# Finer loads of one weight group, one exp moved behind a copy, eight small loads moved one slab on: three edits to a fused attention and feed-forward kernel

## The chip, the cores and the metric

The kernel runs on one core of one Trainium2 chip. The metric is the device time of one execution in microseconds (us). Times are medians of several runs, and ratios carry a 95% interval. The profile comes from one execution, and its times count from the start of that execution's span.

## The reference, cut to what matters

```
q_s = softmax(q, over the head dimension);  k_s = softmax(k, over the sequence)
kv  = einsum('bhsd,bhse->bhde', k_s, v)            # 64 x 64 per head
x   = einsum('bhsd,bhde->bhse', q_s, kv)           # 8 batches x 576 tokens x 512
h   = x @ w_in                                     # 512 -> 2048
out = (h * sigmoid(beta * h)) @ w_out              # 2048 -> 512
```

The shapes are 8 batches, 8 heads, 576 tokens, 64 per head, all float32. The kernel computes in bf16 with float32 sums. It works in nine slabs of 512 tokens: the first 512 tokens of each batch, then the eight remainders of 64 together.

## The kernel before

PE is the matmul engine, ACT does exp and some copies, DVE and POOL do casts, sums and scaling, and SP issues nearly all loads in one queue. A helper turns recorded operations into five instruction streams and puts in the semaphore waits; each stream runs in the order in which the program adds to it. Names in the profile lines: QF, KF and VF are queries, keys and values as loaded, EQ and EK their exps, VB the cast values, QT the transposed queries, KVC the key-value products; XT is the attention output, the input of the first layer; O2S and WST are staging buffers, WIN and WOUT the weights in bf16, GT the hidden layer, PS the banks that take PE's sums, and QRF and EQR belong to the remainder queries.

The weights of the first layer come in four column groups `c` of four row blocks `m`. They land in float32 staging buffers and are cast to bf16:

```
for c in range(4):
    for m in range(0, NM, 1 if c < 2 else 2):
        load_win(c, m, 1 if c < 2 else 2)          # groups 0, 1: 256 KB; groups 2, 3: 512 KB
...
def cast_win(c, m, eng):
    add(eng, lambda e: e.tensor_copy(WIN[:, m, 512 * c:512 * c + 512], STAGE[c][:, m, :]),
        r=[SKEY[c][m]], w=[("win", c, m)])
```

While slab 0 is in its second layer, batch 1 is prepared for slab 1. A list of pieces of work is put between the matmuls, each at a given slot:

```
todo = [(107, lambda: go(t_steps(1, (0, 1), (1,), ACTE))),            # transposes of queries
        (107.1, lambda: cast_v(1, 0, ACTE)),
        (111.1, lambda: scale_wout(14, 2)), (119.1, lambda: (exp_kc(1, 2), exp_kc(1, 3))),
        (118, lambda: kv_half(1, (7, 0), 0)),
        (124, lambda: out_half(1, (1, 2), 0)), (124.5, evacs)]         # copies to XT 0 and 1
... # then slab 1 begins:
at(0, 0, 3)               # three matmuls with XT block 0
kv_half(1, (7, 0), 2)     # 36 small key-value products of the last two head pairs
at(1, 0, 3)
at(0, 3, 5)
out_half(1, (7, 7, 7, 0), 2)
```

`exp_kc(1, 3)` is the exp of batch 1's last keys. `out_half` ends with the two copies XT<-PS, block 0 on DVE and block 1 on ACT. The remainder queries of two batches come in eight loads of 32 KB (`load_qrem`). Two such sets are issued in slab 1, ahead of the store of slab 1 and the loads of batch 4:

```
for hp in range(2, 4):
    norm_main(2, hp, 1, POOL if hp == 2 else DVE)
t_dma(2, 2, 2)
load_qrem(2)
load_qrem(0)
```

The softmax here doesn't subtract the row's maximum and nothing guards it: scores larger than these inputs give would overflow.

## Time and profile before

| | before |
|---|---|
| time, median of the first 3 runs | 280.04 us (279.76 to 280.06) |
| span of the profiled execution | 278.2 us |
| PE busy | 273.0 us (98%) |
| first weight matmul of slab 0 | 13.62 us |
| matmul after the 36 products | 45.48 us |

The matmul lengths are modelled, so a busy PE has to be read from starts: in an unbroken stretch, 512-column matmuls start 0.216 us apart. The prediction below shows the lines that carry the argument.

### The profile page before, as it was taken

The numbers are of one execution on the slowest core, as the hardware profiler recorded it, in microseconds if no ns is written. First come the engines' busy times: TensorE is split into PE (matmuls) and PEld (weight loads), VectorE is DVE, ScalarE is ACT, GpSimd is POOL, SyncE is SP. The second block draws the span as 40 slices with busy tenths as digits, with TensorE's granted clock in tenths as the row PEclk, the third lists the DMA queues.
The fourth block names the chain that finished last, engine by engine and source line by source line (L and its number), as shares of the span: only waits on it lengthen the run. The fifth ranks groups of instructions, "written<-read, shape, count | busy, mean of one in ns | idle before, by whom it ended". The sixth has DMA issues, their size and how long they took to land.

```text
span 278.2 us, 4609 instructions
## 1 busy us (share of the span) xinstructions
PE 273.0 (98%) x1921; PEld 130.7 (47%) x1921; DVE 101.7 (37%) x205; ACT 165.4 (59%) x239; POOL 33.9 (12%) x51
## 2 busy tenths in 40 slices
PE   7999999999999999999999999999999999999995
PEld 3544443444445444545454545454444444444443
DVE  4744685007560139115720564036603300110012
ACT  5868467899478837783579447953751175027500
POOL 2630131036100203230003000000000000000000
PEclk9999999999999999999999999999999999999999
DMA  7999999999349999971599134002600120011022
GB/s 240 371 391 401 388 383 264 374 389 240 46 145 318 317 326 367 355 168 25 167 386 193 32 151 94 2 4 95 150 0 2 67 84 2 0 75 75 2 75 76
DMA packets 43229, 50.38 MB, mean 181 GB/s; under 512 B 22084, under 2 KB 30532, under 8 KB 42056
## 3 DMA queue, kind: packets, MB, share of 16 engines
q1 hardware_dynamic: 42368, 49.16, 54.8%
q10 hardware_dynamic: 840, 0.93, 1.2%
q8 instruction: 15, 0.25, 0.4%
q14 instruction: 6, 0.05, 0.0%
HBM read 36.71 MB, written 9.44 MB: 166 GB/s over the span
## 4 chain that ended last, share of the span: by engine, by line
PE 83%; DMA 11%; SPq 3%; DVE 1%; ACT 0%; issue 0%
PE PS L370 83%; DMA KF<-in_k_dram 4%; DMA WST<-in_moe_w_out_dram 4%; DMA WST<-in_moe_w_in_dram 3%; SPq L250 2%; SPq L567 1%; DVE WOUT L560 1%; SPq L291 0%; ACT EK L320 0%; ACT XT L457 0%; SPq L296 0%; DVE WIN L571 0%; SPq L556 0%; DVE O2S L722 0%; SPq L147 0%
## 5 line engine op out<-in xcount | busy, mean ns | idle before, releaser
L646 ACT ACTIVATE GT<-PS,BETA 128x512 bf16<-128x512 f32 x144 | 96.4, 690 | 62.0 <-PE PS L370 61.9
L370 PE MATMUL PS<-WOUT,GT 128*128 128x512 bf16 (+2 forms) x592 | 127.8, 373 | 0.0
L370 PE MATMUL PS<-XT,WIN 128*128 128x512 bf16 x576 | 126.7, 379 | 0.5 <-ACT XT L457 0.3
L370 PEld LDWEIGHTS PS<-XT,WIN 128*128 128x128 bf16 x576 | 60.3, 106 | 64.3 <-ACT XT L457 0.9
L370 PEld LDWEIGHTS PS<-WOUT,GT 128*128 128x128 bf16 x592 | 56.3, 98 | 66.5 <-DVE WOUT L560 1.1
L701 DVE COPY O2S<-PS 128x512 f32<-128x512 f32 x33 | 22.6, 687 | 124.3 <-PE PS L370 124.3
L355 POOL CAST VB<-VF 128x576 bf16<-128x576 f32 x29 | 20.5, 708 | 88.4 <-DMA VF<-in_v_dram 87.1
L336 DVE TENSOR_REDUCE QS<-EQ 128x8 f32<-128x512 bf16 (+1 forms) x22 | 20.1, 911 | 17.3 <-ACT EQ L312 17.3
L320 ACT ACTIVATE EK<-KF 128x1152 bf16<-128x1152 f32 (+1 forms) x19 | 18.4, 1005 | 5.4 <-DMA KF<-in_k_dram 5.1
L457 ACT CAST XT<-PS 128x512 bf16<-128x512 f32 x14 | 7.6, 587 | 22.1 <-PE PS L370 21.9
L312 ACT ACTIVATE EQ<-QF 128x512 bf16<-128x512 f32 x32 | 17.6, 615 | 4.1 <-DMA QF<-in_q_dram 4.1
L338 DVE TENSOR_TENSOR EQ<-EQ,QI 128x1024 bf16<-128x1024 bf16 (+1 forms) x13 | 14.8, 1141 | 0.4
L457 DVE CAST XT<-PS 128x512 bf16<-128x512 f32 x14 | 9.1, 686 | 12.4 <-PE PS L370 12.4
L338 POOL TENSOR_TENSOR EQ<-EQ,QI 128x512 bf16<-128x512 bf16 x9 | 9.4, 1042 | 27.6 <-DVE QI L337 27.2
L370 PEld LDWEIGHTS PS<-VB,EK 64*64 64x64 bf16 x576 | 6.7, 107 | 4.4 <-issue 2.5
L370 PE MATMUL PS<-VB,EK 64*64 64x65 bf16 x576 | 8.1, 194 | 0.2 <-POOL VB L355 0.2
L646 ACT ACT_TABLE_LOAD x5 | 6.4, 1283 | 0.1
L370 PE MATMUL PS<-QT,KVC 64*64 64x512 bf16 x64 | 6.3, 384 | 0.1
L370 PE MATMUL PS<-XT 128*128 128x512 f32 x6 | 4.5, 900 | 1.5 <-DVE XT L226 1.5
L337 DVE RECIPROCAL QI<-QS 128x8 f32<-128x8 f32 (+1 forms) x22 | 5.0, 226 | 0.8
L320 ACT ACT_TABLE_LOAD x4 | 5.1, 1283 | 0.1
L560 DVE TENSOR_SCALAR WOUT<-O2S,RB 128x512 bf16<-128x512 f32 x8 | 3.8, 526 | 2.6 <-DMA O2S<-in_moe_w_out_dram 2.6
(51 smaller groups left out, 66.3 us busy)
## 6 DMA issues: line engine op xcount, KB each, us to landing
out_dram<-O2S SPq DMA_DIRECT2D x8, 1024.0 KB, 4.6
QF<-in_q_dram SPq DMA_DIRECT2D x30, 256.0 KB, 5.8
KF<-in_k_dram SPq DMA_DIRECT2D x6, 1152.0 KB, 8.0
VF<-in_v_dram SPq DMA_DIRECT2D x6, 1152.0 KB, 10.8
KF<-in_k_dram SPq DMA_DIRECT2D x8, 288.0 KB, 8.0
VF<-in_v_dram SPq DMA_DIRECT2D x8, 288.0 KB, 8.2
WST<-in_moe_w_in_dram SPq DMA_DIRECT2D x8, 256.0 KB, 8.0
O2S<-in_moe_w_in_dram SPq DMA_DIRECT2D x4, 512.0 KB, 11.7
```

The costliest lines, as they stand in the source:

```text
L250: add(engs[c % len(engs)], lambda e, a=a, o=o: e.dma_start(o, a), w=[(name, i, hp) for hp in range(c * n, c * n + n)], slot=f"{name}{i}_{c}")
L312: add(ACTE, lambda e, o=o, a=a: e.activation(o, a, ACT.Exp), r=[("qf", i, hp, x) for x in ((2, 3) if hp % 2 else (hp // 2,))], w=[("eq", i ...
L320: add(ACTE, lambda e: e.activation(o, a, ACT.Exp), r=[("kf", i, h) for h in range(hp, hp + n)], w=[("ekc", i, h) for h in range(hp, hp + n)])
L336: add(DVE, lambda e: e.tensor_reduce(s_, a, AX.X, ALU.add), r=ks, w=[("qs", i, hp0)])
L337: add(DVE, lambda e: e.reciprocal(v_, s_), r=[("qs", i, hp0)], w=[("qi", i, hp0)])
L338: add(eng, lambda e: e.tensor_tensor(a, a, vb, ALU.mult), r=ks + [("qi", i, hp0)], w=ks)
L355: add(eng, lambda e: (e.copy if eng == ACTE else e.tensor_copy)(o, a), r=[("vf", i, hp), ("vone", i)], w=[("vb", i, hp, h) for h in ((0, 1 ...
L370: add(PE, lambda e: e.matmul(o, l, r_, start=start, stop=stop, tile_position=tp), r=r, w=w, bank=[bk])
L457: add(eng, lambda e, eng=eng, bk=bk, hp=hp: (e.copy if eng == ACTE else e.tensor_copy)(XT[i][:, hp, :], PS[bk][:, :]), r=[("ps", bk)], w=[ ...
L560: add(DVE, lambda e, f=f: e.tensor_scalar(WOUT[:, f, :], STAGE[f // 4][:, f % 4, :], RB[:, f:f + 1], None, ALU.mult), r=[SKEY[f // 4][f % ...
L646: add(ACTE, lambda e: e.activation(GT[:, f, :], PS[bk][:, :], ACT.Silu, scale=BETA[:, f:f + 1]), r=[("ps", bk), "beta"], w=[("gt", f)], ba ...
L701: add(eng, lambda e: (e.copy if eng == ACTE else e.tensor_copy)(O2S[t % 2][:, u, :], PS[bk][:, :]), r=[("ps", bk)], w=[("o2", t % 2, u)], ...
```

## The change

The intent is to let PE start the third weight group sooner, to get the second XT block out ahead of an exp that PE does not need yet, and to clear the load queue ahead of batch 4.

```
-            for m in range(0, NM, 1 if c < 2 else 2):
-                load_win(c, m, 1 if c < 2 else 2)
+            for m in range(0, NM, 1 if c < 3 else 2):
+                load_win(c, m, 1 if c < 3 else 2)
...
-                        (111.1, ...), (119.1, lambda: (exp_kc(1, 2), exp_kc(1, 3))),
+                        (111.1, ...), (119.1, lambda: exp_kc(1, 2)), (124.2, lambda: exp_kc(1, 3)),
...
                 if t == 2:
+                    load_qrem(0)
                     load(5)
...
                     load_qrem(2)
-                    load_qrem(0)
```

I call them part 1, part 2 and part 3.

More of the change, by code (lines that the diff above doesn't have):

```diff
@@ L753, in bass_efficient_attn_shen__then__act_swish_beta_kernel @@
                         (107.1, lambda: cast_v(1, 0, ACTE)),
-                        (111.1, lambda: scale_wout(14, 2)), (119.1, lambda: (exp_kc(1, 2), exp_kc(1, 3))),
+                        (111.1, lambda: scale_wout(14, 2)), (119.1, lambda: exp_kc(1, 2)), (124.2, lambda: exp_kc(1, 3)),
                         (118, lambda: kv_half(1, (7, 0), 0)),
```

## The prediction

> **What bounds the kernel now.** I read the busy shares and the 40 slices first. They say that the matmul engine (PE) works almost without a break, at full clock, and that the loads fill the first sixth of the span.
>
> ```profile
> PE 273.0 (98%) x1921; PEld 130.7 (47%) x1921; DVE 101.7 (37%) x205; ACT 165.4 (59%) x239; POOL 33.9 (12%) x51
> PEclk9999999999999999999999999999999999999999
> DMA  7999999999349999971599134002600120011022
> ```
>
> PE is busy 273.0 of 278.2 us, so no change outside PE can give more than the few microseconds in which PE waits. Next I read the chain of waits, its end:
>
> ```profile
> 33.05 10.25 DMA KF<-in_k_dram
> 43.30 0.02 issue
> 43.32 0.68 ACT EK L320
> 44.00 0.48 ACT XT L457
> 44.49 0.05 issue
> 44.53 230.75 PE PS L370 x1612
> ```
>
> From 44.53 to 275.28 us the chain is PE alone. Before that it is data arriving: the last key load of batch 1 lands at 43.30, its exp runs on ACT, then a copy XT<-PS, and only then PE goes on. So a saving must come either from this junction or from a wait inside the 230.75 us. To see what PE waits for, I read the timeline by engine.
>
> ```profile
> 20.75 0.76 DVE L571 CAST WIN<-O2S 128x512 bf16<-128x512 f32 x2 [0.77 <-DMA O2S<-in_moe_w_in_dram]
> 21.33 7.07 PE L370 MATMUL PS<-XT,WIN 128*128 128x512 bf16 x32 [0.19 <-ACT GT L646]
> 36.77 2.16 POOL L338 TENSOR_TENSOR EQ<-EQ,QI 128x512 bf16<-128x512 bf16 x2 [3.19 <-DVE QI L337]
> 37.52 0.75 PE L368 MATMUL PS<-IDB,EQ 128*128 128x128 bf16 x8
> 38.10 2.64 PE L370 MATMUL PS<-WOUT,GT 128*128 128x512 bf16 x11
> 43.90 0.38 PE L370 MATMUL PS<-XT,WIN 128*128 128x512 bf16 x1
> 43.91 0.57 ACT L457 CAST XT<-PS 128x512 bf16<-128x512 f32 x1
> 44.05 0.67 POOL L355 CAST VB<-VF 128x576 bf16<-128x576 f32 x1 [0.71 <-DMA VF<-in_v_dram]
> 44.53 0.61 PE L370 MATMUL PS<-XT,WIN 128*128 128x512 bf16 x2 [0.26 <-ACT XT L457]
> 45.07 0.48 PE L370 MATMUL PS<-VB,EK 64*64 64x65 bf16 x36
> 45.48 1.25 PE L370 MATMUL PS<-XT,WIN 128*128 128x512 bf16 x5
> 95.17 2.86 POOL L355 CAST VB<-VF 128x576 bf16<-128x576 f32 x4 [24.37 <-DMA VF<-in_v_dram]
> 97.64 0.92 PE L370 MATMUL PS<-VB,EK 64*64 64x65 bf16 x72
> ```
>
> Columns are start, duration, engine, line, operation, count, and in brackets the idle time before with its releaser. Three places matter: the break before 21.33, the junction at 44.5, and the slightly long group at 97.64.
>
> **What the Trainium skill says.** "TensorE: Matmul & The Clock Gate", Back-to-back issue gap, gives N/2.4 + 2.5 ns for one warm matmul, 215.8 ns at 512 columns, and also calls about 131 ns the sustained spacing. The trace agrees with the first: a slab's 64 matmuls take 13.98 us, (13.98 - 0.38)/63 = 0.216 us each, 0.38 being the modelled length of one. I use 0.216 for every matmul. "DMA: Bandwidth & Descriptors", Why a DMA increments its semaphore by 16 and not by 1, says that the engines of one DMA finish independently and only the full count means that the data is there. So the first block of a two-block load cannot be used before the second has landed. The trace agrees: the third group's two-block loads let their casts start at 20.75 and 22.10, 1.35 us apart, two casts back to back each time. The same page, Queues, rings and completion order, says that each DMA engine consumes descriptors in ring order. The last four loads of batch 1 land accordingly, at 41.95, 42.66, 43.30 and 44.03 us, about 0.69 us apart: a backlog drained in order of issue. "Perfetto Trace Analysis", Tensor Engine Instruction, calls ACT a strict FIFO. The trace agrees: the copy that PE wants, whose input was ready near 43.1, starts at 43.91, behind the exp.
>
> **Part 1, third weight group by single blocks.** It removes two loads of 512 KB and adds four of 256 KB; bytes and casts are the same. SP issues two more, about 0.45 us each as the eight earlier ones (3.89 us for 8), while it is ahead of the transfers anyway: it is through at 13.2 us and its next load waits until 16.46 for a buffer. The two-block loads land 1.35 us apart, so one block is 0.675 us. The first block lands at about 20.73 - 0.675 = 20.06, its cast ends 0.43 later at 20.5, and the weights are there before PE wants them. PE without a wait would start at 14.93 + 28 x 0.216 = 20.98; it starts at 21.33. The profile names ACT GT, but those banks had been freed by 19.5; the first cast ends at 21.18, and this is what PE waited for. So part 1 gives about 0.3 us at 21.33 (0.35 less perhaps 0.05 at the fourth group, whose third block is cast at 25.24 while PE then wants it near 25.3).
>
> Does it last? PE would reach the transposes of batch 1 at 37.2 instead of 37.52. The second four read what POOL multiplies first from 36.77; two such take 2.16 us, so the first is done about 37.85. Even now the eight take 0.75 where 0.64 would be unhindered. PE goes on at 38.10 either way. That POOL step hangs on a DVE sum that starts at 35.71, behind the scaling of output weights (landed near 34.1) and an exp of queries (landed at 34.9): data arriving, which part 1 does not hasten. A second such gate follows, the scaling of output weights 14 and 15 at 41.09 and DVE's work up to 42.64. So I count **0 of part 1's 0.3 us** in the end.
>
> **Part 2, the last key exp behind the copy.** Same instructions, two swapped on ACT. The copy's input is ready at about 43.1 (PE's group at 42.59 lasts 0.50), so it can run 43.1 to 43.7 and the exp 43.6 to 44.3. PE's three matmuls with the first XT block then go at 43.90, 44.12 and 44.38 (the third needs a bank that DVE empties by 44.33). They end at 44.60; with the 0.11 that a change to small matmuls costs here (46.67 after 45.48 + 5 x 0.216 = 46.56) the 36 key-value products could start at 44.71. Their last operand is the value cast on POOL, 44.05 to 44.72, after a load that landed at 44.03. Handover from POOL takes some 0.06, so they go from about 44.78 instead of 45.07. The next matmul moves from 45.48 to 45.19: **0.29 us saved**, and the new wait is the value load. After it everything is PE, so it stays to the end. The transposed queries needed next land at 41.24 + 3.8 = 45.04, in time for 46.4.
>
> **Part 3, eight remainder loads a slab later.** SP spends 12.30 us from 68.22 on sixteen of them, and the store and the loads of batch 4 queue behind, so half removed lets those start about 5 us earlier (81.22 to about 76.5). This frees two things. The values of batch 4 land before 95.15, so that their four casts, now ending at 98.03, no longer touch the products at 97.64: the following group starts 0.73 us later there, against 0.65 at 71.73, so **0.08 us saved**. And ACT's 1.04 us wait for keys before 92.14 goes, off the path. What it adds is a later arrival of the data that ACT exponentiates at 96.3 to 97.5. The eight loads would be issued after two transposes, which occupied SP for 9.31 us from 85.60; starting 5 us earlier they end near 90.5, the loads near 96, landing near 98. ACT may wait about 2 us, which delays the two XT copies at 98.83; PE needs them at 104.11, so there are about 4 us of room.
>
> **Sum:** 280.04 - 0.29 - 0.08 = 279.67, about 279.7 us.
>
> **Rivals.** (a) Part 1's 0.3 us survives, which needs the loads at 34 to 44 us to land earlier too. For it: a freed buffer lets SP issue the next weight load 0.35 earlier. Against it: issue to landing is about 11 us there, so the queue, not the issue, sets the landing, and the DMA row is at nine tenths throughout. Time then 279.4. (b) The value load takes the place of the exp more fully than I think, for example because four small transfers drain more slowly than two and all later landings slip by 0.2 to 0.3. For it: single blocks of the first groups show one gap of 1.58 us (casts at 17.82 and 19.40). Against it: other neighbours are 0.66 apart, the same rate as the pairs. Time then 279.9 to 280.0. (c) Part 3 makes ACT the bound in the fourth slab. It needs the remainder loads to land after 102 us, 4 us later than estimated. It would cost 0.3 to 1 us, so 280.0 to 280.7.
>
> **Range and chances.** The three runs of before lie within 0.30 us. I give (a) about 15%, (b) 20%, (c) 5%. The range 279.35 to 280.05 covers my sum, (a) and most of (b). Two per cent is 5.6 us, more than all of PE's idle time, and I see no mechanism that would add as much. So faster 0.01, same 0.98, slower 0.01.
>
> **What would show it.** Right: no PE break before the third weight group, but the transposes still end so that PE resumes near 38.1; the copy XT<-PS ahead of the last exp on ACT; the 36 products at about 44.8, released by POOL's cast; the PE stretch to the end the same 230 us less 0.1; the four value casts of batch 4 well before 97 us. Wrong: PE resuming at 37.8 after the transposes (then rival a), the last value load landing after 44.2 (rival b), the XT copies of the third slab later than 103 (rival c).

## The result, and the profile after

In the first measurement the changed kernel took 279.69 us (279.03 to 280.33, 6 runs) and the kernel before 279.70 (279.34 to 280.06, 6 runs). The ratio is 0.9996, interval 0.9979 to 1.0013. A ratio is the mean time of one kernel's fast runs over that of the other's in the same rounds, so it is not quite the ratio of the medians. The time is the predicted one, but this measurement alone shows no gain: the interval is 1 us wide and the forecast saving 0.37 us. That the time itself was met so closely is luck: the forecast was counted down from 280.04, the median of the first three runs of before, and over six runs that median was 279.70. Two more sets of rounds (below) gave 0.9983 and 0.9982.

The timeline of the changed kernel at the places that the prediction names, with the columns as there:

```profile
15.19 13.12 PE L370 MATMUL PS<-XT,WIN 128*128 128x512 bf16 x60
36.91 2.16 POOL L338 TENSOR_TENSOR EQ<-EQ,QI 128x512 bf16<-128x512 bf16 x2 [3.10 <-DVE QI L337]
37.50 0.91 PE L368 MATMUL PS<-IDB,EQ 128*128 128x128 bf16 x8
38.25 2.64 PE L370 MATMUL PS<-WOUT,GT 128*128 128x512 bf16 x11
43.27 0.59 ACT L457 CAST XT<-PS 128x512 bf16<-128x512 f32 x1 [0.47 <-PE PS L370]
43.75 0.69 ACT L320 ACTIVATE EK<-KF 128x576 bf16<-128x576 f32 x1
44.04 0.88 PE L370 MATMUL PS<-XT,WIN 128*128 128x512 bf16 x3
44.23 0.67 POOL L355 CAST VB<-VF 128x576 bf16<-128x576 f32 x1 [0.74 <-DMA VF<-in_v_dram]
44.84 0.58 PE L370 MATMUL PS<-VB,EK 64*64 64x65 bf16 x36
45.36 1.25 PE L370 MATMUL PS<-XT,WIN 128*128 128x512 bf16 x5
90.74 2.87 POOL L355 CAST VB<-VF 128x576 bf16<-128x576 f32 x4 [20.22 <-DMA VF<-in_v_dram]
97.53 0.83 PE L370 MATMUL PS<-VB,EK 64*64 64x65 bf16 x72
98.33 0.63 ACT L326 ACTIVATE EQR<-QRF 128x512 bf16<-128x512 f32 x1 [2.50 <-DMA QRF<-in_q_dram]
98.86 1.05 ACT L457 CAST XT<-PS 128x512 bf16<-128x512 f32 x2
```

The 28 and 32 matmuls of before are one unbroken group of 60. The eight transposes take 0.91 us instead of 0.75, so PE waits there a little longer. The copy stands ahead of the exp on ACT. From the start of the last value cast to the matmul after the products it is now 45.36 - 44.23 = 1.13 us; before it was 45.48 - 44.05 = 1.43. The four value casts of batch 4 run from 90.74 instead of 95.17. ACT now waits 2.50 us for a remainder load, and PE does not notice: the XT copies start at 98.86, at 98.83 before.

The end of the chain of waits of the changed kernel:

```profile
36.91 1.05 POOL EQ L338
37.97 0.05 issue
38.01 0.40 PE PS L368 x4
38.41 236.59 PE PS L370 x1677
```

Before, the chain went from data to PE at 44.53. Now it does so at 38.01, at the transposes. The chain shows only the wait that ended last, and the small wait at the products is left inside the long piece.

In this execution the loads landed later than in the profiled one of before (last value cast at 44.23 against 44.05) and PE began the first weight group later (13.89 against 13.62). The start-up differs by as much as the effect that I look for. So I compare the kernels by intervals inside a trace, and the times only over many runs.

### The profile page after: what moved, and what is told of

Same layout as the page of the kernel before. It is cut to its first block, busy times and chain, and to the rows that moved or that the text cites. A ratio compares the mean times of both kernels' runs of the same rounds, so it can differ in the third digit from the quotient of the medians.

```text
span 278.0 us, 4612 instructions
## 1 busy us (share of the span) xinstructions
PE 273.2 (98%) x1921; PEld 131.0 (47%) x1921; DVE 102.0 (37%) x205; ACT 165.6 (60%) x239; POOL 33.5 (12%) x51
## 4 chain that ended last, share of the span: by engine, by line
PE 85%; DMA 8%; SPq 4%; DVE 1%; issue 0%; POOL 0%; POOLq 0%
PE PS L370 85%; DMA O2S<-in_moe_w_out_dram 4%; DMA O2S<-in_moe_w_in_dram 4%; SPq L567 2%; SPq L250 2%; DVE WOUT L560 1%; POOL EQ L338 0%; SPq L291 0%; DVE QS L336 0%; SPq L296 0%; DVE WIN L571 0%; PE PS L368 0%; DVE O2S L722 0%; DVE QI L337 0%; POOLq L147 0%
## 5 line engine op out<-in xcount | busy, mean ns | idle before, releaser
L370 PE MATMUL PS<-XT 128*128 128x512 f32 x6 | 5.5, 1084 | 1.5 <-DVE XT L226 1.5
```

The source lines that it names most:

```text
L370: add(PE, lambda e: e.matmul(o, l, r_, start=start, stop=stop, tile_position=tp), r=r, w=w, bank=[bk])
```

## The experiments

There were twelve runs of ten kernels, each with 5 rounds, in three sets of four. The record names another chip for each set (9, 7 and 11), so times are best compared within a set. Three marks from each trace tell nearly all: **A**, the start of the first weight matmul of slab 0; **V**, the start of POOL's last value cast of batch 1, which follows the landing at once; **K**, the start of the matmul after the 36 products. From K to PE's last group of matmuls it is 215.55 to 215.81 us in all of the profiles in this table, so K decides the end to within 0.26 us; most of that rest arises in the third and fourth slab (below). V stands for the loads that come last. Without part 2 it is the key load that PE waits for, and it lands about 0.7 us before the values.

| profile | part 1 | part 2 | A | V | K | K - A | K - V |
|---|---|---|---|---|---|---|---|
| before | no | no | 13.62 | 44.05 | 45.48 | 31.86 | 1.43 |
| changed | yes | yes | 13.89 | 44.23 | 45.36 | 31.47 | 1.13 |
| p1_only | yes | no | 14.16 | 43.93 | 45.31 | 31.15 | 1.38 |
| p2_only | no | yes | 13.68 | 44.17 | 45.30 | 31.62 | 1.13 |
| p3_only | no | no | 13.78 | 43.70 | 45.11 | 31.33 | 1.41 |
| after_again | yes | yes | 14.42 | 43.60 | 45.22 | 30.80 | 1.62 |
| after_third | yes | yes | 13.70 | 44.33 | 45.46 | 31.76 | 1.13 |
| exp_twice | no | no | 14.11 | 43.98 | 45.96 | 31.85 | 1.98 |
| light_all | yes | yes | 13.65 | 42.09 | 44.45 | 30.80 | 2.36 |
| light_no_p1 | no | yes | 14.08 | 41.86 | 44.88 | 30.80 | 3.02 |
| whole3 | reversed | no | 13.73 | 43.66 | 45.74 | 32.01 | 2.08 |
| light_whole3 | reversed | yes | 13.85 | 42.09 | 46.14 | 32.29 | 4.05 |

### Each part alone, and all three again (first set)

**p1_only**: the edit is the first hunk of the change.

> Part 1 alone (third weight group by single blocks). My theory: the PE break before the third weight group (0.35 us in the kernel before) goes, PE enters the transposes of batch 1 earlier, waits there for POOL and resumes where it did; from the start of the last value cast of batch 1 to the 36 products stays 1.02 us (44.05 to 45.07 before). Time: 0 us against before, ratio 1.000. Rival a (the 0.3 us survives): PE resumes 0.3 earlier after the transposes and the time falls by 0.3 us, ratio 0.9990. Rival b (four small loads drain slower): the last value load lands 0.2 later or more.

Measured: 279.81 us against 279.89, ratio 0.9997 (0.9980 to 1.0015). K - V stays at 1.38, so what follows the value load is as before. One V of 43.93 cannot settle rival b, since V scatters by 0.7 us: it is 44.23 and 44.33 in two profiles of the changed kernel, about where the prediction put the sign of rival b. An interval inside the trace can: from the last cast of the fourth weight group to V it is 24.66 to 43.93 = 19.27 us here, 19.24 in before, and over the profiles with all data 19.17 to 19.65 with single blocks and 19.17 to 19.58 with pairs. Nothing later is slowed by the single blocks, so rival b falls. The transposes took 0.61 us: PE began late, at 14.16, and did not wait there, so this profile does not show the expected wait for POOL. Rival a is not supported, but this run alone does not exclude it: the interval holds 0.9990.

**p2_only**: the edit is the second hunk.

> Part 2 alone (last key exp behind the copy). My theory: copy XT<-PS before the exp on ACT, from the start of the last value cast to the matmul after the 36 products 1.14 us instead of 1.43, and this 0.29 us stays to the end: time about 0.3 us less, ratio 0.9990. Rival (the exp itself becomes the wait): the products wait for ACT, the interval stays at 1.4 us and the time at 0.

Measured: 279.51 us, ratio 0.9986 (0.9969 to 1.0003). K - V is 1.13, the same as with all parts, 0.30 less than in the kernel before. The end of the chain of waits now names the value load, where in before it named the key load, the exp and the copy:

```profile
32.95 11.17 DMA VF<-in_v_dram
44.12 0.05 issue
44.17 0.68 POOL VB L355
44.85 0.04 issue
44.90 230.00 PE PS L370 x1607
```

So the rival, that the exp becomes the wait, falls by the trace; the interval of the time alone still holds 1. The trace has something that I had not expected. This kernel loads the third group by pairs, as before, and yet PE has nearly no break there:

```profile
13.68 1.04 PE L370 MATMUL PS<-XT,WIN 128*128 128x512 bf16 x4
14.99 13.19 PE L370 MATMUL PS<-XT,WIN 128*128 128x512 bf16 x60
20.53 0.76 DVE L571 CAST WIN<-O2S 128x512 bf16<-128x512 f32 x2 [0.77 <-DMA O2S<-in_moe_w_in_dram]
```

Sixty unhindered matmuls take 59 x 0.2157 + 0.38 = 13.11 us; here it is 13.19. PE began at 13.68 instead of 13.62, and the casts began at 20.53 instead of 20.75. The 0.35 us break in the profile of before was largely an accident of that execution: an early PE and a late load. In p3_only, exp_twice and light_no_p1, which also load by pairs, the 60 take 13.12: no break at all.

**p3_only**: the edit is the third and fourth hunks.

> Part 3 alone (eight remainder loads a slab later). My theory: the products of the third slab go without the POOL wait (0.65 us to the next group instead of 0.73), the junction at 45 us is as before (1.43 us), time 0.08 us less, ratio 0.9997, which these rounds cannot tell from 1. ACT waits about 2.5 us for the moved loads near 96 us and this costs nothing. Rival c: the wait on ACT reaches PE, and the time rises by 0.3 us or more.

Measured: 279.61 us, ratio 0.9987 (0.9972 to 1.0002), which is more than 0.08 us but holds 0.9997 too. K - V is 1.41, so the junction is as before. The products of the third slab take 0.65 us to the next group, as they do in every profile with part 3. Without it the figure was 0.73 (before), 0.81 (p1_only), 0.74 (exp_twice), 0.65 (p2_only and whole3). So part 3 saves 0 to 0.16 us, depending on where PE stands when the values of batch 4 land: the four casts end 0.20 and 0.23 us after the start of the products in the two profiles with 0.65, and 0.39 to 0.47 after it in the other three. From K to the last group of matmuls it is 215.55 to 215.66 us in the seven profiles with part 3 and 215.56 to 215.81 in the five without. ACT waits 2.96 us for the moved loads, and its XT copies start at 99.05; they are needed near 104. Rival c falls.

**after_again**: the changed kernel.

> All three parts, the changed kernel again in the same rounds. My theory: the sum of the parts, 0.29 + 0.08 = 0.37 us less than before, ratio 0.9987; from the start of the last value cast to the matmul after the products 1.14 us. Rival (no effect at all, only scatter of the start): ratio 1.000 and an interval that holds 0.9987 out.

Measured: 279.44 us, ratio 0.9983 (0.9965 to 1.0001). The expected 0.9987 lies in the interval; so does 1.000, only just. K - V is not 1.14 here but 1.62, a miss. PE began very late, at 14.42, and from there to K it needed 30.80 us. This was not the value load but PE's own work. It suggested the rule that the later runs test: K is the later of A + 30.80 and V + 1.13 (V + 1.4 without part 2).

### Doubling one cost, and taking data away (second set)

**exp_twice**: in the kernel before,

```
- (119.1, lambda: (exp_kc(1, 2), exp_kc(1, 3)))
+ (119.1, lambda: (exp_kc(1, 2), exp_kc(1, 3), <exp of the same keys into a scratch tile>))
```

> The kernel before with the disputed cost doubled: one more exp of the same 128x576 keys into a scratch tile, on ACT between the last key exp and the copy XT<-PS (result unchanged). My theory: ACT's order at this place lies on the path to the end one to one, so the copy and the products move about 0.6 us later (start of the last value cast to the next matmul 2.05 us instead of 1.43), and the time rises by 0.6 us, ratio 1.0021. Rival (the junction has slack, or the time is made up later): the products move but the end does not, ratio 1.000.

```profile
43.23 0.68 ACT L321 ACTIVATE EK<-KF 128x576 bf16<-128x576 f32 x1 [0.68 <-DMA KF<-in_k_dram]
43.81 0.67 ACT L755 ACTIVATE SCR<-KF 128x576 bf16<-128x576 f32 x1
44.39 0.57 ACT L458 CAST XT<-PS 128x512 bf16<-128x512 f32 x1
45.01 0.61 PE L371 MATMUL PS<-XT,WIN 128*128 128x512 bf16 x2 [0.82 <-ACT XT L458]
```

The extra exp puts the copy off by 0.58 us, and PE waits 0.82 us for the copy instead of 0.26. K - V is 1.98, 0.55 more than before. The time is 280.62 us against 279.78; the ratio is 1.0020 (0.9999 to 1.0040), which is 0.56 us. The interval just holds 1, for the set's runs of before held two near 281, which widens it. The trace decides: from V to the last group of matmuls it is 217.79 us (43.98 to 261.77) against 217.21 in before. So the order on ACT lies on the path to the end one to one, and the rival (made up later) falls.

**light_all** and **light_no_p1**: the changed kernel with less to load, and the same without part 1. Their outputs are wrong, which doesn't matter for the times.

```
- load_wout(8)            # 1 MB
+ load_wout(8, 1)         # 256 KB; scale_wout for 8 to 11 reads this block each time
```

> The changed kernel with 768 KB less to load: of output weights 8 to 11 only the first block is loaded and used four times (the result is wrong on purpose). My theory: what holds PE between 37 and 45 us is data arriving, so later loads land about 2 us earlier, the waits there go, and PE gains what it lost in them, 0.6 to 0.8 us: time about 0.7 less than the changed kernel. Rival (something else than data, such as the order of work on ACT or DVE): the loads land 2 us earlier and the time falls by less than 0.2.

> The same with part 1 undone (third weight group by pairs; wrong result on purpose). My theory: with the later gates open, part 1's 0.3 us is no longer taken back, so this one is 0.3 us slower than its twin with part 1; the break of 0.35 us before the third weight group is back. Rival (part 1 never matters, or is lost elsewhere): both take the same time within 0.1 us in the trace from the first weight matmul to the end.

Measured: light_all 279.02 us, ratio to before 0.9964 (0.9943 to 0.9984); light_no_p1 279.29 us, ratio 0.9974 (0.9951 to 0.9997). In light_all V is 42.09, about 2.1 us earlier than in the changed kernel's profile, and K - A falls from 31.47 to 30.80: PE no longer waits for anything between, and the transposes take 0.61 us instead of 0.91. Its last group of matmuls starts at 260.00, against 260.77 to 261.02 in the three profiles of the changed kernel. The times size the gain only roughly, because the changed kernel did not run in this set. The nearest to it on the same chip is kv_one_later (below), with 279.46 us: light_all is 0.44 us lower by the medians. By the medians it is also about 0.4 us below the changed kernel's 279.44 and 279.38 on the other chips. That is less than the 0.6 to 0.8 that I expected and more than the rival's 0.2, but the six runs of each (278.81 to 279.42 and 279.06 to 279.89) overlap, so 0.2 is not excluded by the times. By the rule, once the data is there PE's own 30.80 us decides, and executions in which PE begins late gain nothing. The trace is clearer: PE began as early as in after_third (below; 13.65 and 13.70), and K - A is 30.80 us instead of 31.76. So the waits between 37 and 45 us, where PE has them, are arriving data.

light_no_p1 is 0.27 us slower, just as my theory said, but this is within the noise (the intervals overlap), and the traces do not support the theory. Its own has no break before the third group (60 matmuls in 13.12 us) and the same K - A of 30.80. PE began later in that execution, at 14.08 against 13.65. From A to the last group of matmuls it is 246.35 and 246.41 us: the rival's expectation. The test was void, because there was no break for part 1 to remove.

**kv_one_later**: in the changed kernel,

```
  at(0, 0, 3)
+ at(1, 0, 1)
  kv_half(1, (7, 0), 2)
- at(1, 0, 3)
+ at(1, 1, 3)
```

> The changed kernel with one matmul moved ahead of the 36 products (one matmul with the second XT block, which is copied by then). My theory: the products wait for the last value cast, so a matmul in that gap is free: 0.1 us less than the changed kernel, too little for the times, seen in the trace as start of the last value cast to the fifth following matmul 0.1 us shorter. Rival (the products are not what waits): no change or 0.2 us more.

Measured: 279.46 us, ratio 0.9977 (0.9956 to 0.9999). The order of matmuls differs here, so I count from V to the query products that follow. In the changed kernel it was 46.54 - 44.23 = 2.31; here it is 46.29 - 44.06 = 2.23.

### Making part 1's wait large (third set)

To give part 1's place a wait that every execution has, I turned it round: the third group in one load of 1 MB.

```
- for m in range(0, NM, 1 if c < 2 else 2):      # load_win(c, m, same)
+ for m in range(0, NM, (1, 1, 4, 2)[c]):
```

> The kernel before with part 1 turned round and made larger: the third weight group in one load of 1 MB instead of two of 512 KB, so its first block is usable only when the fourth has landed (about 22.1 us). Theory: PE breaks before the third group by 1.2 to 1.7 us, depending on when it began with the first group; of this the later data waits swallow as much as PE would have waited there anyway (0.35 to 1.05 us in the profiles so far, as 30.80 us of unhindered work from the first group's start to the matmul after the products falls short of it), so the time rises by only 0.3 to 1.0 us, ratio 1.001 to 1.0036. Rival (a wait at this place passes through in full): 1.2 to 1.7 us, ratio 1.0043 to 1.006.

> The same 1 MB load in the kernel with 768 KB less to load and without part 1 (wrong result on purpose). Theory: with the later data waits gone nothing swallows the break, so it passes through in full: 1.2 to 1.7 us more than that kernel with two loads had (279.29 us), about 280.5 to 281.0. Rival (swallowed by something other than data): as in the run with all data, 1 us or less.

The timeline of whole3, then of light_whole3:

```profile
15.03 6.22 PE L370 MATMUL PS<-XT,WIN 128*128 128x512 bf16 x28
21.73 2.11 DVE L571 CAST WIN<-O2S 128x512 bf16<-128x512 f32 x6 [2.12 <-DMA O2S<-in_moe_w_in_dram]
22.30 7.07 PE L370 MATMUL PS<-XT,WIN 128*128 128x512 bf16 x32 [1.05 <-DVE WIN L571]
38.49 0.61 PE L368 MATMUL PS<-IDB,EQ 128*128 128x128 bf16 x8
```

```profile
15.15 6.22 PE L370 MATMUL PS<-XT,WIN 128*128 128x512 bf16 x28
22.13 2.12 DVE L571 CAST WIN<-O2S 128x512 bf16<-128x512 f32 x6 [2.12 <-DMA O2S<-in_moe_w_in_dram]
22.70 7.07 PE L370 MATMUL PS<-XT,WIN 128*128 128x512 bf16 x32 [1.33 <-ACT GT L646]
```

In whole3 PE resumes at 22.30 where it could have at 15.03 + 28 x 0.2157 = 21.07: a break of 1.23 us. The transposes then take 0.61 us, so PE comes late enough to find everything ready, and K - A is 32.01 = 30.80 + 1.21. The break is whole in that sum, but the data waits that other executions have in this stretch are gone. The time is 280.20 us against 280.12, ratio 1.0010 (0.9996 to 1.0024): 0.28 us for a break of 1.23. That is just under the low end of what was expected and excludes the rival's 1.0043. By the rule, with the V of this execution, K would have been 43.66 + 1.4 = 45.06 without the break; it is 45.74, so 0.68 of the 1.23 reached K and the rest was swallowed.

In light_whole3 the break is 22.70 - 21.19 = 1.51 us (the profile names ACT GT as its end, but PE starts 0.57 us after the start of the first cast in both traces, so the load ends it in both), and K - A is 32.29 = 30.80 + 1.49. Against the profile of light_no_p1, K and the last group of matmuls are 1.26 and 1.28 us later. The median is 280.19 us, 0.90 above light_no_p1's 279.29 of another set; by the two ratios to before (1.0010 and 0.9974) it is 1.0 us, and counted from the two medians of before 0.56. That is less than the 1.2 to 1.7 expected, probably because I had not allowed for the start of PE, which no longer matters once the load sets the pace, and which was late (14.08) in the profile of the run with two loads. Across two chips, and with these intervals, the times alone would not separate this from the 0.28 us of whole3. The trace does: by the rule K would have been 13.85 + 30.80 = 44.65 without the break; it is 46.14, so 1.49 of the 1.51 reached K. The two kernels with the 1 MB load take the same time, 280.20 and 280.19, though one loads 768 KB less: once PE is late, the later data has no effect.

**kv_one_again** and **after_third**, in the same rounds:

> The changed kernel with one matmul moved ahead of the products, again, now in the same rounds as the changed kernel. Theory: up to 0.1 us less than the changed kernel in executions where the last value load sets the pace, nothing in those where PE does; 5 rounds cannot resolve that. Rival: slower by 0.2 us.

> The changed kernel a third time, for the mean and the scatter. Theory: 0.2 to 0.4 us less than before, ratio 0.9987 to 0.9993; the matmul after the products starts at the later of two: 30.80 us after the start of the first weight group, or 1.13 us after the start of the last value cast. Rival: ratio 1.000.

Measured: kv_one_again 279.26 us, ratio 0.9975 (0.9962 to 0.9988); after_third 279.38 us, ratio 0.9982 (0.9967 to 0.9997). The changed kernel's interval now excludes 1. Its profile has A + 30.80 = 44.50 and V + 1.13 = 45.46, and K is 45.46, so the rule holds. From V to the query products it is 2.32 in after_third and 2.10 in kv_one_again. So the version with one matmul ahead of the products is clear of the kernel before in both its sets; its 0.1 to 0.2 us over the changed kernel is seen in the traces, and the times do not resolve it.

## Why the prediction was right, and where its reading was not

**Time, 279.7 us with a saving of 0.37.** The time was 279.69, 279.44 and 279.38 us in three sets. The plain mean of the three ratios, 0.9996, 0.9983 and 0.9982, is 0.9987, which is 0.36 us. Only the third set's interval excludes 1 by itself. That the first set met 279.7 to 0.01 us was luck, as said above: its saving was 0.12 us by the means.

**Part 2, 0.29 us.** Right in mechanism and size, by the traces; the time of part 2 alone, 0.9986 (0.9969 to 1.0003), fits but holds 1. K - V is 1.38 to 1.43 in the three profiles without part 2 or an added cost (before, p1_only, p3_only) and 1.13 in the three with it where the value load sets the pace. The wait that takes its place is the value load, as predicted; the chain of p2_only names it. What the prediction did not say is that this is the gain only while V sets the pace: in after_again, where PE began at 14.42, PE's own 30.80 us ended later than V + 1.13.

**Part 1, 0 us in the end.** The number is consistent with the runs: 0.9997 alone, with an interval that does not exclude 0.3 us. The mechanism of being swallowed by later data is shown on an enlarged scale by whole3 and light_whole3: breaks of 1.23 and 1.51 us at this place, of which by the rule 0.68 and 1.49 us reach K. The gate that decides is the last one, though, and not the transposes that the prediction names first: in p1_only PE did not wait at the transposes, and K was still V + 1.38. And the step "PE without a wait would start at 14.93 + 28 x 0.216 = 20.98; it starts at 21.33", taken as a property of the kernel, was one execution's. The four other profiles that load this group by pairs show 0.08, 0, 0 and 0. So in most of these executions part 1 has nothing to remove.

**Part 3, 0.08 us.** Right as an order of size: 0 to 0.16 us by the trace. Its side effect came as estimated: the loads were issued from 90.52, the exp that needs them waited 2.50 us, and nothing behind it moved. The measured ratio 0.9987 of part 3 alone is more than the trace accounts for; its interval holds both, and I leave this open.

**The transposes.** "PE goes on at 38.10 either way" came out as 38.25 in the changed kernel, 0.28 after POOL's first product ended near 37.97, in an execution whose loads were some 0.15 later. In after_again, with a late PE, there was no wait there.

**Small readings of the prediction that do not hold.** The DMA row stands at 9 up to slice 10, which is 70 us or a quarter of the span, not a sixth; 3.89 us for 8 loads is 0.49 each, not 0.45; and the transposes without a wait take 0.61 us, not 0.64. None of them enters the sum.

**Left unexplained.** In the fourth slab the products take 0.65 to 0.80 us to the next group in different profiles of any of these kernels, 0.78 in the one of before. The profile names no releaser for it.

## What to carry to other kernels

A wait seen in one profile belongs to that execution until a second profile shows it: compare the start marks of several traces before putting a value on a break of 0.3 us. Where two chains meet, here PE's own work and arriving data, write down the later of the two as a rule with measured constants; it tells at once which edits can add up. To test a saving that is too small for the scatter of the times, enlarge it, and remove what is suspected of swallowing it, in a kernel whose result may be wrong.

## What the Trainium skill lacked or had wrong

- "TensorE: Matmul & The Clock Gate", Back-to-back issue gap, calls about 131 ns the sustained spacing of 512-column matmuls. Here 64 with their weight loads take 13.98 us in slab after slab, 0.216 us each, as its formula for one has it.
- "DMA: Bandwidth & Descriptors", Bandwidth, gives the rule to batch DMAs to 1 MiB or more for three quarters of the peak. Its table is for loads issued from GpSimd; in SP's queue with a backlog the rule did not show: in the changed kernel blocks of 256 KB of the third group let their casts start at 20.29, 20.96, 21.65 and 22.33, 0.68 us apart, which is 385 GB/s, and pairs of 512 KB let theirs start 1.35 apart in the kernel before, the same rate.
- No page that I read has the scatter of the start: in three profiles of the changed kernel alone PE's first weight matmul began at 13.70, 13.89 and 14.42 us, and the cast of batch 1's last values at 44.33, 44.23 and 43.60.
